# One group's softmax sums moved from ones-products to accumulating transfers, with a new hand-written order

## The chip, the cores and the metric

The kernel runs on one core of a Trainium2 chip. A core has five engines, each with its own queue of instructions, which it works through in order: PE (TensorE, matrix products), DVE (VectorE), ACT (ScalarE), POOL (GpSimd) and SP (SyncE, which here only issues transfers). Transfers run on 16 DMA engines. Instructions wait for each other by semaphores only. The metric is the device time of one execution in microseconds, the median of several runs.

## The reference

Two layers. The first is attention in which a query sees only the keys that fall to the same of 16 centroids; the second is a long convolution over the sequence by FFT, between two gates.

```python
# attention: batch 4, heads 8, seq 768, head_dim 64, 16 centroids per head
q_assign = argmax(einsum(q_n, c_n)); k_assign = argmax(einsum(k_n, c_n))
mask = q_assign[:, :, :, None] == k_assign[:, :, None, :]
scores = where(mask, scale * q @ k.T, -1e9)
attn = exp(scores - max); attn = attn / (sum(attn) + 1e-9)
x = (attn @ v) as (batch, seq, 512)
# gated convolution: d_model 512
x1, x2, x3 = split(x @ w_proj)
y = x1 * irfft(rfft(x2) * rfft(filter)) * x3
out = y @ w_out
```

## The kernel before

**Groups, pairs, key blocks.** The 32 heads of the four batches are worked through in 8 *groups* `n` of 4 heads (half a batch each); a group has two *pairs* `pr` of 2 heads. For a pair the 768 keys come in 6 *blocks* `sk` of 128. For each block PE makes the scores, keys on the partitions and the queries of both heads along the row, in three parts of 512 columns (`sc`); ACT turns each into exponentials (`p`, `exp`); PE multiplies the block with V into an accumulating pair of PSUM banks (`pv`, eight products, line 661). The mask is part of the score product: the one-hot rows of the assignments are extra rows of its operands (`aug`), copied there by small transfers `aug<-ohT` on SP (line 482). The assignments themselves come from `routing`: a similarity product (`sim`), then a run of DVE instructions up to `ohT`.

**The sums of the exponentials.** They have to be summed over all keys, over the six blocks and over the 128 partitions. Over the blocks: the first two are added in three thirds (`part`, line 678, on DVE or POOL), the other four one after another by DVE (`acc`, line 682, 128 x 1536 values). The accumulator `T.acc[os]` has one buffer for each pair of a group, so the same pair of the next group overwrites it. Over the partitions there are two ways:

- *late* groups (0, 1 and 7 before): a product with a matrix of ones on PE (`den`, line 695, four products, each in two instructions), a copy with the epsilon (`total`, lines 701 to 704), and for all but the very last pair two small transfers through DRAM, `dd<-den` and `dn<-dd` (lines 707, 709).
- other groups (2 to 6 before): a tree of three accumulating transfers issued by POOL (line 715): rows 64 to 127 are added onto rows 0 to 63, then 32 onto 32, then 16 onto 16, each waiting for the one before. The 16 rows left go to DRAM (`dd<-acc`, SP, line 719), come back spread over 128 partitions in pieces of 48 bytes (`dp<-dd`, SP, line 721), and DVE adds the 16 and the epsilon (`gather`, lines 725 and 726).

After either way DVE takes the reciprocal (line 728), SP writes it to DRAM (`dr<-dn`, line 729) and reads it back broadcast over 64 partitions twice (`rb<-dr`, line 732), and DVE scales the output by it into `xT` (line 761). The very last pair does this on PE instead (lines 743 to 761).

**The second layer.** When both groups of a batch have their `xT`, `hyena(b)` starts: projections (`U`, line 798; `G`), spectrum, inverse transform (`I`), output product (`W`). Its parts lie between the products of the following groups; those of the last batch lie behind all attention.

**The order.** `build` makes some 1,940 operations with their dependencies. The order of all of them is written out in `ORDER`, a word each: the letter is the engine (P, A, V, G, S for PE, ACT, DVE, POOL, SP), the number is the operation's number in `build`, and behind the colon stand the PSUM banks. An operation that may run on two engines gets its engine from there. The instructions are issued in this order, engine by engine, and the semaphores follow from the data that instructions share. The due times and costs in `build` do not act on the program once `ORDER` is given. The tables of the filter (`tables`) are loaded into the buffers of `y` and `y2`; `hot` warms up PE at the start with 16 products that read `y`.

Of the kernel before, what the change touches and what calls it, by code (L numbers as in the profile page):

```python
# [34 lines left out]
FIRST = 2  # L35
# [89 lines left out]
A35 V0 G18 S45 A46 P14:0 G29 S47 V22 P6:1 G20 S48 P5:2 G28 P11:3 S52 P1:4 G23 P2:5 V36 V53 S51 P16:6 G34 V37 P13:7 V59  # L125
G17 S49 V38 P4:0 V54 A39 A40 P7:1 V60 G19 V55 S50 P10:2 P3:3 G24 V61 P15:4 P9:5 P12:6 G137 V21 V56 P68:7 A66 A63 P70:0
V62 A57 P8:1 G33 S121 V41 A69 P74:2 G27 A58 P76:3 A64 G30 S124 A71 V26 P42:4 A77 V75 G65 S123 G72 P140:5 A67 P142:6
V43 P146:1 V143 S122 P82:7 G25 V141 G32 V44 S120 A73 P80:0 V83 G31 S135 A79 P102:3 V81 G78 P144:2 S134 P138:6 A103 V84
P96:5 A145 G136 S130 P100:4 V85 A97 P94:7 A101 V86 S131 P108:0 A95 G133 V87 A105 S127 P106:3 V88 A139 S126 V89 G104
P149:2 A99 P249:5 S128 G132 P251:4 A151 V93 V91 A250 V90 P243:7 A252 V92 S125 P183:6 V109 P245:5 A244 G98 V107 A184  # L130
S129 P185:0 P187:7 V150 G253 A186 P190:3 S288 V110 P192:6 P194:2 A188 V147 P200:0 V111 S287 A195 P202:7 V112 A246
P204:2 V199 A191 P189:45 V113 A193 V197 A201 A203 V198 P208:3 P210:6 A205 P212:0 V114 P216:7 P196 A211 V207 A209 A213
P218:2 P220:6 A254 P224:3 V148 P226:0 G154 V115 P206 A217 A219 V119 A118 P228:1 V153 P263:7 A116 V155 P214 V117 A221
V215 A248 P293:2 P222 A227 A294 V157 A229 P255:6 V223 A225 P257:0 P295:2 A264 P297:1 P300:3 A258 P261:7 A256 P302:0
V158 P230 A298 V160 A301 A262 V231 A296 P304:6 P310:1 S352 P312:3 A305 P267:72 S291 A303 V156 A232 S292 V159 A311
P233:6 S285 V269 A259 G162 P314:0 V268 S290 P318:1 A313 P299:45 V270 A315 G161 S289 A266 V234 P320:2 S286 P322:7 A319
V271 G152 P163:3 A323 S242 P171:0 A260 P164:6 S235 V272 P326:1 V273 G307 P328:7 A165 P306 A327 V166 A167 G358 P330:1
V274 A169 P316 G353 A331 V275 G309 A329 P334:3 P172:1 A321 V168 S278 P336:7 A175 G356 P177:2 V276 S280 V170 P324 A335
G308 S277 A173 V176 S279 V174 P419:361 S236 G247 A337 A181 V317 G357 A265 P338:0 P178:7 S453 A339 P332 S454 A421 V420
A422 V325 P359:0 A179 P361:1 P363:3 P340 A362 A360 V182 G426 A364 P366:6 V237 P368:1 A342 V180 P370:0 S238 G355 P376:3  # L140
P378:7 A371 V333 P365:45 S282 G354 A369 S455 A367 P380:2 A379 S283 P384:0 V374 P386:1 A381 P388:6 S281 P392:7 V341
A377 P372 S284 A387 S239 A385 P394:2 A389 S240 V375 P396:3 P343:1 A397 V373 A395 P427:063 V383 A393 A344 S345 P400:2
P402:7 A429 P404:1 V391 P382 A430 A428 A401 P461:0 A405 V399 P463:3 P465:6 A403 P390 A466 S346 A425 V407 P468:2
P435:17 S456 A464 V241 P470:6 P472:3 P398 A471 V437 A462 G476 V436 A473 P478:6 V438 P480:0 P482:1 P486:7 A481 P488:3
V347 P406 V439 A469 S348 A433 S458 V440 A483 P409:0 S418 V441 G475 A408 S459 P490:2 A489 P494:1 P467:45 V442 S460 A495
A487 S349 V443 G477 A410 P474 A479 A491 S446 V444 P496:3 S411 V485 P498:1 P502:7 A497 P701:062 S448 A434 S445 A424
V431 S447 P484 A499 V493 S350 S452 P504:3 P506:1 S457 P492 A505 V423 A704 S412 V501 A503 S520 P500 A507 S449 A703 S451
P639:3 V509 P508 A640 S738 A702 P641:7 V413 P643:1 A510 G708 P511:3 S414 A642 G432 P646:0 A644 V512 P648:2 P650:6 A647
G706 P656:7 S513 P658:1 A649 P660:3 P645:45 S450 V351 A657 A661 V653 A651 S416 P664:0 P666:2 A659 P668:7 V655 S415
P672:3 P674:6 A669 P676:1 V707 P652 A673 S514 V654 A677 A665 V663 P709:731 A675 A667 P680:0 V671 P682:6 S741 P684:2  # L150
A681 P662 A685 A711 V515 A683 V679 P743:0 S516 P670 A710 S740 A744 A712 S735 P745:2 V417 P747:6 P750:0 P752:1 P717:37
V687 A753 A746 S518 A748 S517 P754:1 A714 V718 P760:2 G689 P678 S736 V719 A755 G758 V720 S700 A751 P686 V721 P762:6
P764:3 A688 V722 P768:7 P770:1 P772:0 A761 V723 G757 P749:45 A765 A769 V724 P776:2 A771 P778:3 P780:7 P756 A779 V759
A763 V519 A705 G690 P766 V725 A781 V726 P521:1 S728 V767 S804 P523:3 A522 S729 A777 P531:6 S727 V525 A773 S732 V524
P526:7 A532 S730 V775 G691 P784:1 S739 P786:2 P528:0 A787 S742 A527 P533:3 A713 S734 V529 P788:6 P564:2 S733 V534 A789
S737 P774 V535 A785 G537 A715 V530 S692 A565 P805:7 V536 P807:6 P809:1 P812:3 A808 V539 P814:0 P816:2 A810 P782 V783
A806 A815 P822:6 A817 P824:1 P826:7 V538 A823 P830:0 P790 A813 V791 A831 A827 P540:2 S866 A792 P543:6 G819 V542 S693
P867:307 A825 V541 S731 V544 G821 P811:45 A869 V545 A870 V546 G793 A868 P548:1 V547 A873 P832:2 P834:6 V549 G716
P551:0 A833 P838:3 V550 P818 A835 G820 V552 A839 V553 P840:7 P842:2 V829 P875:163 A843 P556:0 V554 A877 S906 P828 A841
V837 A876 G794 A878 P846:2 P566:7 A847 V557 G555 P848:1 P850:3 V694 P909:6 P559:2 A910 P836 V695 V560 A851 S696 A871  # L160
V558 S903 G562 P911:6 V567 P568:3 S907 A912 V561 P913:0 P883:76 A569 G795 V845 S908 A879 S904 A849 P570:2 A914 S698
V884 G563 V885 P916:3 P918:1 P579:0 V886 A919 P920:6 P926:7 A580 P928:1 V887 A917 P844 A921 V853 A929 S796 P572:03
A927 P852 A573 V888 G855 V574 P930:6 G872 V575 P934:1 P581:7 A931 V889 A854 G576 S797 P936:0 P583:3 V582 A882 S901
P938:6 V890 P915:45 A584 A937 V891 G923 A939 P942:7 P922 A880 V571 S896 V577 A943 S894 V925 A874 P587:30 S697 V892
P585:6 V578 G856 S895 A588 A935 P932 S893 V586 G924 A881 S902 V589 V590 P944:2 S899 P946:7 V798 P950:1 P952:6 A947
S905 P594:0 V933 P596:3 A595 A951 P940 A953 V799 V941 S800 G857 A945 P954:7 S970 P1089:0 P598:1 A955 S898 A1090 V699
P1091:6 P1093:2 P1096:7 P1098:0 P948 V949 A1099 A1092 S801 A1097 P1100:0 S802 P1106:6 A1094 P956 V957 S858 A1107 A1101
P1108:7 P600:2 A958 V592 G959 P1110:6 V591 A1109 P1114:0 P1095:45 A599 G593 A1111 V601 V597 S859 P1116:7 P1118:1
P1151:623 A1117 G1105 A1115 A1119 P609:7 A1152 V1154 S1186 P602:01 A1153 V1103 S1187 P1159:236 V1104 A603 S897 A1158
V605 G1155 S900 V604 P1102 A1161 V1113 G960 S1191 A1162 S1190 A1160 P1122:0 P1124:1 A1123 P1167:23 S1192 V803 A610  # L170
G607 P1126:6 V1168 P1112 A1127 G606 V860 A1125 V1169 A1156 P1130:0 G961 P1132:7 V861 V1170 P1134:6 S862 A1131 P1193:1
P1195:2 P1197:3 P1120 A1196 V1121 A1135 A1198 P1200:0 A1133 P1202:2 V1171 P1204:6 P1210:3 A1194 P1212:7 P1128 A1203
S864 V1172 A1201 S1188 V1129 A1211 P611:1 S962 A1163 P1214:2 S863 P1218:0 A1166 P1220:3 V612 P1136 S1185 V1173 A1213
A1205 V1137 P1222:1 A1215 P613:7 A1138 P617:62 S963 A1221 P1199:45 V608 A618 S1189 A614 V1174 P1226:3 P1228:7 P1206
A1227 V620 G1208 A1223 V1175 A1219 P1230:3 V619 A1229 P1216 G1139 S1178 V1176 A1231 G622 S1177 A1157 V964 P1234:1
S1183 P615:0 A1164 V965 G621 P1224 S966 V616 S1180 V1207 S1179 P1236:2 V1209 P1232 A1237 V865 A1235 A1165 P1238:6 V623
P1325:730 S967 A1239 V1217 S968 G1140 P1317:216 S1150 A1328 S1182 A1326 V1225 A1327 S1254 P1240 A1320 S1184 A1319
S1181 A1318 P1255:0 V1233 P1257:3 P1259:7 A1256 P626:1 A1260 A1258 P624:2 P1262:6 V969 G1141 P631:0 A625 A627 V1241
P1264:7 P629:3 A1265 A1263 P981:2 V630 G1243 P971:1 V1321 P973:7 G1324 A972 S1142 A982 P983:6 G1323 V975 A1242 S628
V974 P976:3 A632 V984 P978:1 A977 V985 P1266:2 P1272:7 V979 P1014:0 A1267 S1143 V980 P1274:3 P1276:6 S1352 V987  # L180
P1280:2 A1275 P1261:45 G1244 A1273 V986 S1358 A1281 V988 A1015 S1356 P1282:1 P1284:3 V989 P990:7 A1283 S1351 P1288:2
G1269 P993:0 V991 A1289 P1016:1 S1355 V992 A1285 P1018:2 V994 A1277 G1270 S1316 P1020:7 V1017 A1019 V995 P998:3 G996
P1290:6 V1144 P634:1 V1145 V997 P1001:2 S1146 A635 P1006:0 V999 G1271 A1291 P1268 V1002 V1000 G1004 P636:1 V1003
P1292:6 V1021 P1296:3 G1005 P1009:2 V1007 P1298:7 P1278 V1010 A1299 G1245 A637 V1279 A1293 P1300:7 S638 P1029:1 A1301
# [1009 lines left out]
```

## Time and profile before

| | |
|---|---|
| median of 3 runs | 366.29 us (366.25 to 366.62) |
| the profiled execution's own time | 366.52 us |
| its span, first to last instruction | 364.7 us |
| granted TensorE clock, mean | 0.996 |
| busy: PE, DVE, ACT, POOL | 353.9, 339.3, 271.1, 137.1 us |

Busy time is the time in which an engine has an instruction under way. The products of PE are pipelined and their ends are modelled, so a busy PE may hide short waits; the chain of waits, followed back from the last instruction, tells what each step was released by. In the views by stretch each line gives start and end in us, the length, and then for PE, PEld (weight loads), DVE, ACT and POOL the busy time with the number of instructions, then the granted clock, the DMA engines' busy share and GB/s. In the groups by line, the figures after the bar are busy us, the mean ns of one instruction, and the idle time before them with what ended it.

### The profile page before, as it was taken

To read this page: it belongs to the slowest core of one execution; us is meant where nothing else is said; L and a number is where in the kernel's file an instruction comes from. 1 tells how busy PE (TensorE), PEld (TensorE's weight loads), DVE (VectorE), ACT (ScalarE), POOL (GpSimd) and SP (SyncE) were. 2 spreads that over 40 slices of the span, in tenths; PEclk is the share of its full clock that TensorE was granted. 3 is DMA by queue.
4 is the path that set the end of the run, shared out by engine and by line. 5 is a ranking of instruction groups with operands and counts; after the bars stand their busy time and mean duration, and the time that the engine had idled before them with its cause. 6 is when DMAs were issued, how large, how long until landed. Compare 5 with 4: busy or idle time off the path is not lost.

```text
span 364.7 us, 8483 instructions
## 1 busy us (share of the span) xinstructions
PE 353.9 (97%) x3254; PEld 198.8 (55%) x3254; DVE 339.3 (93%) x470; ACT 271.1 (74%) x502; POOL 137.1 (38%) x167
## 2 busy tenths in 40 slices
PE   8799999999999999999999999999999999999994
PEld 4445445454555555665565555555655556475771
DVE  8899889998999999989987999999999999999992
ACT  5999989789878777898987667789969826532232
POOL 8930841122131644344143463432340363045500
PEclk9999999999999999999999999999999999999998
DMA  9990999165576568678667948375755640410214
GB/s 171 226 248 14 218 180 179 26 166 132 120 134 147 102 108 129 130 148 151 131 125 193 174 111 155 43 156 56 178 80 155 89 61 17 162 43 2 117 59 173
DMA packets 88004, 45.69 MB, mean 125 GB/s; under 512 B 76488, under 2 KB 82012, under 8 KB 87964
## 3 DMA queue, kind: packets, MB, share of 16 engines
q1 hardware_dynamic: 84076, 35.16, 40.9%
q0 software_dynamic: 2960, 9.77, 18.6%
q8 instruction: 25, 0.41, 0.5%
q10 hardware_dynamic: 928, 0.23, 0.3%
q14 instruction: 15, 0.12, 0.1%
HBM read 31.59 MB, written 7.40 MB: 107 GB/s over the span
## 4 chain that ended last, share of the span: by engine, by line
PE 77%; DVE 9%; ACT 8%; DMA 3%; issue 2%; SPq 0%; DVEq 0%
PE bank L69 33%; PE pair L661 26%; PE bank L798 6%; PE bank L551 4%; ACT p L650 3%; DVE acc L682 3%; PE bank L583 2%; DMA dn<-dd 2%; PE bank L1015 2%; ACT aug L246 2%; ACT p L647 2%; PE bank L67 2%; DMA aug<-ohT 1%; PE bank L695 1%; PE bank L470 1%
## 5 line engine op out<-in xcount | busy, mean ns | idle before, releaser
L661 PE MATMUL pair<-p,vraw 128*64 128x385 f32 x768 | 140.4, 488 | 0.0
L650 ACT ACTIVATE p<-bank 128x512 f32<-128x512 f32 x192 | 108.5, 614 | 18.0 <-PE bank L69 15.6
L682 DVE TENSOR_TENSOR acc<-p,acc 128x1536 f32<-128x1536 f32 x64 | 112.1, 1751 | 2.1
L661 PEld LDWEIGHTS pair<-p,vraw 128*64 128x64 f32 x768 | 54.5, 136 | 47.6 <-issue 38.8
L69 PE MATMUL bank<-aug,aug 80*64 80x256 bf16 (+3 forms) x708 | 78.9, 327 | 1.3 <-DMA aug<-ohT 0.7
L647 ACT ACTIVATE p<-bank 128x512 f32<-128x512 f32 x96 | 57.8, 613 | 16.8 <-PE bank L69 11.3
L69 PEld LDWEIGHTS <-aug 80*64 80x64 bf16 (+1 forms) x708 | 40.9, 109 | 42.4 <-issue 29.7
L715 POOL DMA_DIRECT2D acc<-acc x30 | 24.1, 805 | 75.1 <-DMA acc<-acc 30.6
L678 POOL TENSOR_TENSOR acc<-p,p 128x512 f32<-128x512 f32 x23 | 29.8, 1298 | 48.6 <-ACT p L650 13.6
L69 PE MATMUL bank<-xT,wpj 128*64 128x384 bf16 x480 | 46.3, 326 | 0.0
L69 PEld LDWEIGHTS <-wpj 128*64 128x64 bf16 x480 | 27.6, 110 | 15.8 <-issue 5.3
L246 ACT CAST aug<-qkP 64x768 bf16<-64x768 f32 x43 | 35.4, 829 | 0.7
L246 ACT COPY qkP<-bank 128x512 f32<-128x512 f32 (+1 forms) x56 | 28.4, 562 | 7.9 <-PE bank L69 5.8
L69 PEld LDWEIGHTS <-y 128*64 128x64 bf16 x480 | 23.8, 110 | 11.5 <-issue 2.4
L822 DVE TENSOR_TENSOR tm<-bank,hm 128x512 f32<-128x512 f32 x44 | 27.9, 682 | 0.9 <-POOL y L826 0.2
L826 POOL TENSOR_TENSOR y<-tm 128x512 bf16<-128x512 f32 x17 | 21.5, 1275 | 13.9 <-DVE tm L822 8.7
L69 PE MATMUL bank<-wout,y 128*64 128x512 bf16 x192 | 23.1, 379 | 0.0
L798 PE MATMUL bank<-wpj,xT 128*64 128x512 bf16 x192 | 21.9, 379 | 0.0
L248 POOL CAST aug<-qkP 64x768 bf16<-64x768 f32 x17 | 13.9, 827 | 20.5 <-DVE dn L728 8.3
L246 ACT COPY ob<-bank 128x512 f32<-128x512 f32 x21 | 12.2, 594 | 11.0 <-PE bank L69 9.3
L900 POOL TENSOR_TENSOR y<-yy,x 128x768 bf16<-128x768 f32 x7 | 13.1, 1868 | 18.7 <-DVE yy L897 13.8
L551 PE MATMUL bank<-ident,qkraw 128*128 128x128 f32 x144 | 18.1, 276 | 0.0
(161 smaller groups left out, 447.2 us busy)
## 6 DMA issues: line engine op xcount, KB each, us to landing
qkraw<-in_k_dram SPq DMA_DIRECT2D x32, 192.0 KB
vraw<-in_v_dram SPq DMA_DIRECT2D x16, 384.0 KB
qkraw<-in_q_dram SPq DMA_DIRECT2D x31, 192.0 KB
rb<-dr SPq DMA_DIRECT2D x30, 192.0 KB
out_dram<-ob SPq DMA_DIRECT2D x11, 512.0 KB
acc<-acc POOLq DMA_DIRECT2D x10, 384.0 KB, 5.0
acc<-acc POOLq DMA_DIRECT2D x10, 192.0 KB, 3.9
wpj<-in_moe_w_proj_dram POOLq DMA_DIRECT2D x4, 384.0 KB, 6.3
```

The lines of the kernel that those rows point to most:

```text
L69: T.nc.tensor.matmul(out[64 * i:64 * i + 64], lhsT[:, 64 * i:64 * i + 64], rhs, start=start, stop=stop)
L246: T.nc.scalar.copy(out, in_)
L551: T.nc.tensor.transpose(bank(h.ids[i // 4])[:, block(i % 4, 2 < i < NT)], raw(ss[i // NT], i % NT), T.ident)
L647: T.nc.scalar.activation(o, ap(h).rearrange("p (a b) -> p a b", a=2), Act.Exp, scale=0.125)
L650: T.nc.scalar.activation(flat(s)[:, lo:lo + 512], ap(h), Act.Exp, scale=0.125)
L661: T.nc.tensor.matmul(o[64 * hp:64 * hp + 64, ch, :385], T.vraw[vs][:, hp, sk * D:(sk + 1) * D], T.p[slots[sk]][:, hp, 384 * ch:384 * ch + ...
L678: alu(e).tensor_tensor(o, x, y, op=Alu.add)
L682: T.nc.vector.tensor_tensor(T.acc[os], T.p[slots[sk]][:, :, :S], T.acc[os], op=Alu.add)
L715: op(("POOL", .8), lambda e, rows=rows: T.nc.gpsimd.dma_start(flat_()[:rows], flat_()[rows:2 * rows], accum_op=Alu.add), te, r=[], w=AK, b ...
L798: T.nc.tensor.matmul(ap(h)[64 * i:64 * i + 64], T.xT[xs][:, kt, tokens(m, i, w_)], T.wpj[:, kt, DM:2 * DM], start=kt == 0, stop=kt == ND - 1)
L822: op(("DVE", .68), lambda e, i=i, cs=cs, r=r, h=h: T.nc.vector.tensor_tensor(T.tm[r][:, cs], ap(h), hmrow(i, (0, 2, 2, 3)[2 * r + cs]), op ...
L826: op({"POOL": 1.3, "DVE": .68}, lambda e, i=i, r=r: alu(e).tensor_tensor(T.y[:, i, r], T.tm[r][:, 0], T.tm[r][:, 1], op=Alu.add if r else ...
```

## The change

Group 1 goes from the ones-product to the accumulating transfers: `FIRST`, below which a group is late, becomes 1. `LATE` writes the other end of that rule in pairs: pair 14 is the first of group 7, as before. `spread` takes the place of `last` where the very last pair is meant. The loads of the filter tables get a dependency on the 16 warm-up products. `ORDER` is new from the first word to the last: the order comes from a search whose picture of SP holds it back behind each load that spreads its rows.

```diff
-FIRST = 2
+FIRST, LATE = 1, 14
...
 ORDER = """
-A35 V0 G18 S45 A46 P14:0 G29 S47 V22 P6:1 G20 S48 P5:2 G28 P11:3 S52 P1:4 G23 P2:5 V36 V53 S51 P16:6 G34 V37 P13:7 V59
...
+A35 V0 G18 S45 A46 P16:0 G20 S48 V22 A47 G27 P11:1 S51 P14:2 G31 P4:3 S52 P1:4 G23 P15:5 V36 V59 S49 P13:6 G19 V37
...
 def tables(got):
...
-                   w=[("f", w_, e_)], byts=131e3 * (2 - e_), kind="load", after=got)
+                   r=[("hot", i) for i in range(HOT)], w=[("f", w_, e_)], byts=131e3 * (2 - e_), kind="load", after=got)
...
-                   r=["back"], w=[("f", w_, 1 + m)], byts=262e3 / m, kind="load", after=got)
+                   r=["back"] + [("hot", i) for i in range(HOT)], w=[("f", w_, 1 + m)], byts=262e3 / m, kind="load", after=got)
...
 def attention(n, pr, sins):
...
-        late = n == NG - 1 or n < FIRST
+        late = n < FIRST or 2 * n + pr >= LATE
+        spread = last and late
         if late:
             h, den_, dk = Bank(), lambda: T.den, ["den"]
...
-        if not last:
+        if not spread:
             if late:
                 op(("SP", .6), lambda e: T.nc.sync.dma_start(T.dd[os][:4, :384], den_()[0:128:32]), te + 2, r=dk,
...
 def hot():
...
-               r=["hot"], w=[h], alloc=h, free=[h])
+               r=["hot"], w=[h, ("hot", i)], alloc=h, free=[h])
```

Engine by engine the new order differs from the old one in where operations run, too. Of the 48 `part` sums DVE gets 33 instead of 25 and POOL 15 instead of 23. The two copies of mask rows of the first group that ACT made go to DVE, and one sum of the filter tables goes from POOL to DVE. A few copies of the second layer go from DVE to ACT, and single sums and products of it change between DVE and POOL. The `den` copy of group 0's first pair goes from DVE to ACT. Batch 0's first projection stands behind the third value product of group 3's first pair; before, it stood behind the third of group 2's second pair. The load of one quarter of `w_proj` (`wpj` 1) stands on POOL behind the tree of group 2's first pair; before, it stood just ahead of group 1's first value product.

210 lines of the change are left out of this document (105 added, 105 removed).

## The prediction

> **What bounds the kernel now.** I read the page first, then the engines' busy time by stretch, then the chain of waits.
>
> ```profile
> span 364.7 us, 8483 instructions
> PE 353.9 (97%) x3254; PEld 198.8 (55%) x3254; DVE 339.3 (93%) x470; ACT 271.1 (74%) x502; POOL 137.1 (38%) x167
> PE 77%; DVE 9%; ACT 8%; DMA 3%; issue 2%; SPq 0%; DVEq 0%
> ```
>
> PE is busy 97% of the span and carries 77% of the chain. DVE, at 93%, is close behind. Where each is short of full shows by stretch (busy us behind each length: PE, PEld, DVE, ACT, POOL):
>
> ```profile
> 0.00:16.00 16.00, 13.27 (x85) 6.49 (x85) 13.16 (x39) 12.03 (x23) 14.13 (x45) 1.00 1.01 196
> 16.00:56.00 40.00, 38.15 (x289) 19.61 (x287) 37.14 (x54) 38.15 (x71) 18.83 (x27) 1.00 0.80 165
> 56.00:316.00 260.00, 259.15 (x2353) 143.95 (x2351) 248.84 (x311) 205.78 (x380) 90.10 (x87) 1.00 0.62 122
> 316.00:365.00 49.00, 43.29 (x537) 28.76 (x533) 40.16 (x69) 15.13 (x30) 14.09 (x10) 0.97 0.23 85
> ```
>
> From 56 to 316 us PE idles under 1 us in 260 and DVE 11. So DVE is a second bound with little room, and both can be full together, as here (the same columns):
>
> ```profile
> 280.00:288.00 8.00, 8.00 (x80) 4.40 (x78) 7.90 (x10) 6.51 (x13) 2.31 (x3) 1.00 0.79 139
> 288.00:296.00 8.00, 8.00 (x68) 4.11 (x66) 7.97 (x14) 4.23 (x9) 3.28 (x4) 1.00 0.33 39
> ```
>
> Now the chain of waits (start, length, what), around the parts that change:
>
> ```profile
> 1.58 6.11 PE bank L1015 x15
> ...
> 48.61 6.45 DMA dn<-dd
> ...
> 55.91 1.67 DVE acc L682
> ...
> 69.42 0.97 DVE sim L588 x2
> 70.43 0.84 PE bank L69 x8
> ...
> 72.57 0.78 PE bank L695 x8
> ...
> 83.31 1.30 PE pair L661 x8
> 85.05 0.78 PE bank L695 x8
> ...
> 159.15 1.30 PE pair L661 x8
> ...
> 235.28 4.17 DMA aug<-ohT
> ```
>
> Three things are to be seen. From 56 to 70 us the chain runs through DVE's sums of exponentials: DVE is the bound there. From 70 us on it is PE nearly without a break, and the two ones-products of group 1 (L695, at 72.57 and 85.05) lie on it in full. At 235 us PE once waits for a mask transfer.
>
> For the working I laid the two orders side by side, gave every instruction the mean duration of its group in the trace, and took 0.05 us off each of DVE's: the durations of its 470 instructions add up to 365 us against 339.3 busy, since they overlap. The orders are then cut at the first value product of a pair. In before's trace these cuts are here (group 1; the last one of group 7), and at 159 us (group 4, in the chain above):
>
> ```profile
> 55.77 1.51 PE L661 MATMUL pair<-p,vraw 128*64 128x385 f32 x8
> ...
> 315.31 1.46 PE L661 MATMUL pair<-p,vraw 128*64 128x385 f32 x8
> ```
>
> From 55.77 to 159 (103.2 us) the order before holds 100.6 us of PE work and 98.7 of DVE work; DVE thus idles 4.5 us. From 159 to 315.3 (156.3 us) it holds 152.8 of PE and 150.2 of DVE.
>
> **The change part by part.** Removed and added, by their groups:
>
> ```profile
> L695 PE MATMUL bank<-acc,ones 128*32 128x384 f32 x48 | 5.1, 496 | 0.0
> L703 DVE TENSOR_SCALAR den<-bank 128x384 f32<-128x384 f32 x2 | 1.1, 552 | 1.1 <-ACT p L647 1.1
> L725 DVE TENSOR_REDUCE dn<-dp 128x12 f32<-128x192 f32 x10 | 4.8, 482 | 0.0
> L726 DVE TENSOR_SCALAR dn<-dn 128x12 f32<-128x12 f32 x10 | 3.4, 339 | 0.3
> L678 DVE TENSOR_TENSOR acc<-p,p 128x512 f32<-128x512 f32 x25 | 17.3, 717 | 0.2 <-ACT p L650 0.2
> L678 POOL TENSOR_TENSOR acc<-p,p 128x512 f32<-128x512 f32 x23 | 29.8, 1298 | 48.6 <-ACT p L650 13.6
> L715 POOL DMA_DIRECT2D acc<-acc x30 | 24.1, 805 | 75.1 <-DMA acc<-acc 30.6
> ```
>
> *PE* loses two ones-products, 2 x 0.78 = 1.56 us, nothing else: 344.6 us of work become 343.0.
>
> *DVE*: both of its den copies go, 2 x 0.55 = 1.1 us (group 1's with the product, group 0's to ACT, which loses group 1's other one). Two gathers come, 2 x (0.48 + 0.34) = 1.6 us. The new order gives DVE 33 of the 48 first sums (L678) instead of 25, 8 x 0.72 = 5.7 us; POOL loses 8 x 1.3. All other exchanges (mask rows and one table sum to DVE; copies, one fold and two products away from it) come to -3.3. In all +3.0 us: less work for the bound, more for the engine beside it.
>
> *Where DVE's load lands* decides. Between the cuts at groups 1 and 4 the new order holds the same PE work, 100.5 us (its dens gone, other work drawn forward), but 102.6 us of DVE work, 3.9 more. From group 4 to the last value product: PE 150.6 (2.2 less), DVE 150.5 (0.3 more). Behind it PE has 44.0 against 43.4, and DVE less. Up to group 1's cut the two orders have the same PE work, and DVE 52.3 against 52.1: no change, at a bound of 0.7 us either way, about what PE waits between 41 and 54 us now.
>
> *The sum* then has one unknown, i, DVE's idle time from group 1 to group 4. That stretch takes 102.6 + i in place of 103.2 if DVE sets it, and not less than PE's 100.5 with waits. Behind it I keep PE's 3.5 us of waits, so 2.2 us are saved, and the end costs 0.65. The change is i - 0.6 - 2.2 + 0.65 = i - 2.15 us. Its bounds: 0.5 (DVE 7.97 of 8 in the row at 288) and 4.5, what it idles now. I take 1.5, nearest the full rows, since 1.1 of the 4.5 is the den copy's own wait for ACT (L703) and goes with it. That gives -0.65 us: 366.52 of the profiled execution (span 364.7 and 1.8 around it) becomes 365.9; it stands 0.23 above the median of 366.29, so the time forecast is 365.6.
>
> *POOL and the DMA queues* get six accumulating transfers, with their landing times (KB, median us), and SP's waits behind them:
>
> ```profile
> acc<-acc POOLq DMA_DIRECT2D x10, 384.0 KB, 5.0
> acc<-acc POOLq DMA_DIRECT2D x10, 192.0 KB, 3.9
> acc<-acc POOLq DMA_DIRECT2D x10, 96.0 KB, 3.7
> ...
> wpj<-in_moe_w_proj_dram POOLq DMA_DIRECT2D x4, 384.0 KB, 6.3
> ```
> ```profile
> SPq L719 <- DMA acc<-acc: 18.6, 5, 8.8
> ...
> SPq L721 <- DMA dd<-acc: 9.1, 6, 2.6
> ```
>
> Six issues cost POOL 6 x 0.8 = 4.8 us, which its eight lost sums (10.4) pay for; POOL is 38% busy. The tree takes 5.0 + 3.9 + 3.7 = 12.6 us from issue to last landing, and the sum leaves the accumulator with dd, at most 2.6 us later. The accumulator alternates between pairs, so the same pair of the next group may write it only then. In the new order 18.8, 18.5 and 18.6 us of PE work lie between a tree's first issue and that next write, for group 1's two pairs and group 2's first: 3.3 us above 15.2. Hence cost nothing; without that cover DVE, which then holds most of these first sums, stands still. The two new dp loads hold SP as now; behind that of group 1's second pair stand the masks of group 3, with 3.2 us in between. One projection weight's load moves from just before group 1's first value product to behind the tree of group 2's first pair on POOL; 10.6 us of PE work lie between it and the first projection, against 6.3 to land. The first projection of batch 0 itself moves 12.3 us of PE work later, behind the longer way of group 1's sums. The `hot` edges tell only the order what the stored data demand anyway: the warm-up products end at 7.7 us (chain), the tables are wanted later, nothing. `LATE` and `spread` give for 8 groups exactly what stood there.
>
> [...]
>
> **Rivals.** *DVE becomes the bound in groups 1 to 3.* Slower. Place: its queue between 56 and 159 us. It decides from i = 2.15 on; where its idle stays at 4.5, the change is +2.35: 368.6 us. For it: the chain already runs through DVE from 56 to 70 us, and 3.9 us are added to 4.5 of room. Against: the full rows at 280 to 296.
>
> *A tree is late.* First to third issue on POOL, an ordinary tree and the slowest:
>
> ```profile
> 243.15 0.81 POOL L715 DMA_DIRECT2D acc<-acc  x1 [6.67 <-DVE acc L682]
> ...
> 252.79 0.77 POOL L715 DMA_DIRECT2D acc<-acc  x1 [3.52 <-DMA acc<-acc]
> ```
> ```profile
> 196.97 1.00 POOL L715 DMA_DIRECT2D acc<-acc  x1 [5.21 <-PE bank L69]
> ...
> 203.63 0.76 POOL L715 DMA_DIRECT2D acc<-acc  x1 [3.88 <-DMA acc<-acc]
> 205.94 2.50 POOL L678 TENSOR_TENSOR acc<-p,p 128x512 f32<-128x512 f32 x2 [1.54 <-ACT p L647]
> ...
> 214.35 0.75 POOL L715 DMA_DIRECT2D acc<-acc  x1
> ```
>
> 9.6 and 17.4 us; the new order leaves 10.8 to 11.9. A tree as slow as the second, 6.4 us late against the 11.0 of group 1's second pair, outruns the cover of 3.3 by 3.1 and holds DVE's first sums, and on SP group 3's masks: 365.6 + 3.1 = 368.7. It decides from 4.0 us of lateness on (3.3 + 0.65). Against: it was held by POOL's own sums, and the new order keeps these out of the three early trees save one.
>
> *It is hidden anyway*: DVE takes back what PE is spared (i = 2.15), 366.3.
>
> *All of it is had*: i at 0.5 and group 6's wait of about a microsecond at 235 us gone too (its masks now have 3.9 us of PE work ahead of the score instead of 2.8): 365.6 - 1.0 - 0.5 = 364.1.
>
> **How the numbers follow.** Forecast (365.6, own range 365.0 to 366.2) 0.46; all of it 0.13; hidden 0.09; DVE the bound 0.21; a tree late 0.11. A measurement of this kernel tells 0.2%, 0.73 us, from no change. The forecast's centre lies at that edge: 0.28 of its 0.46 falls below 365.56, 0.18 within. So faster 0.28 + 0.13 = 0.41; same 0.18 + 0.09 = 0.27; slower 0.32. The range goes from 364.2, just above the case that has it all, to 368.2, which takes in most of DVE's case and a tree late by less than the slowest, and leaves out the far end of both.
>
> **What would show it.** Right: the L695 group shrinks from 48 to 32 products, 36 accumulating issues, L678 at 33 on DVE and 15 on POOL; DVE busy near 342 us, between 248 and 252 of 256 to 260 in the long middle stretch; PE's waits of group 1 gone from the chain. Wrong: PE idle that grows by over 2 us between 56 and 160 us, with the chain on DVE (the first rival) or on acc<-acc, dd or aug<-ohT transfers (the second); or group 6's masks waiting as before. A head that reaches group 1's first value product more than 0.7 us off 55.8 would undo the first term.

## The result, and the profile after

| | before | after |
|---|---|---|
| median, us | 366.42 (366.18 to 367.33, 9 runs) | 369.60 (367.33 to 373.37, 9 runs) |
| the profiled execution's own time, us | 366.52 | 373.12 |
| its span, us | 364.7 | 371.3 |
| busy PE, DVE, ACT, POOL, us | 353.9, 339.3, 271.1, 137.1 | 357.6, 340.5, 272.4, 132.0 |

The ratio of after to before is 1.0065 [1.0039, 1.0091], which is 2.4 us: slower, by 3.2 us in the medians of the table. The ratio leaves out the two longest executions of after (373.12 us, the one profiled, and 373.37), which lie over 1.5% above its fastest; the other seven have a median of 368.41 us. The forecast was 365.6 us, the range ended at 368.2. Another profiled execution of the same kernel, at 370.8 us (run 1 below), has its losses at the same places.

The page of after, its first lines, shares of the chain, and groups:

```profile
span 371.3 us, 8500 instructions
...
PE 357.6 (96%) x3249; PEld 207.6 (56%) x3249; DVE 340.5 (92%) x475; ACT 272.4 (73%) x508; POOL 132.0 (36%) x164
...
PE 83%; ACT 9%; DMA 3%; DVE 2%; issue 1%; SPq 1%; POOL 0%; DVEq 0%; ACTq 0%
...
L716 POOL DMA_DIRECT2D acc<-acc x36 | 28.7, 798 | 110.0 <-DMA acc<-acc 50.5
...
L678 POOL TENSOR_TENSOR acc<-p,p 128x512 f32<-128x512 f32 x15 | 19.1, 1275 | 25.8 <-ACT p L647 6.8
L678 DVE TENSOR_TENSOR acc<-p,p 128x512 f32<-128x512 f32 x33 | 21.4, 684 | 6.7 <-ACT p L650 5.5
```

(After's lines stand one higher than before's from the ones-product on: L716 is the old L715.) The change does what it says: 36 accumulating issues, first sums 33 on DVE to 15 on POOL, 32 ones-products left (L696). DVE's share of the chain fell from 9 to 2%. But PE is busy 3.7 us longer with 1.56 us less to do. By stretch, after and then before (length, then busy PE, PEld, DVE, ACT, POOL, the granted clock, DMA share, GB/s):

```profile
16.00:56.00 40.00, 36.95 (x260) 17.59 (x261) 35.62 (x52) 36.73 (x69) 14.44 (x22) 0.96 0.84 172
56.00:104.00 48.00, 45.94 (x368) 23.48 (x364) 43.34 (x44) 42.46 (x79) 12.83 (x14) 0.96 0.69 133
104.00:122.00 18.00, 16.03 (x111) 8.14 (x109) 16.89 (x20) 10.17 (x20) 3.41 (x5) 0.91 0.80 139
122.00:320.00 198.00, 197.96 (x1860) 119.23 (x1858) 189.16 (x253) 152.41 (x282) 74.90 (x71) 1.00 0.63 123
```
```profile
56.00:104.00 48.00, 47.90 (x392) 23.80 (x390) 45.49 (x46) 41.74 (x80) 9.48 (x10) 1.00 0.57 127
104.00:122.00 18.00, 18.00 (x160) 10.04 (x156) 17.70 (x21) 14.92 (x29) 4.62 (x6) 1.00 0.54 123
122.00:316.00 194.00, 193.26 (x1808) 110.11 (x1807) 185.65 (x246) 149.12 (x274) 76.00 (x73) 1.00 0.64 121
```

All is lost ahead of 122 us. Behind it PE does not wait in 198 us; group 6's mask wait is gone as well. Ahead of it PE idles 7.1 us in 106 (3.05, 2.06 and 1.97), and the granted clock is 0.91 to 0.96 where it was 1.00.

To add up both I use one measure below, **lost time**: from the start of a value product (L661) in the trace I take the time that all PE instructions ahead of it need at their undisturbed length (in all 344.6 us before, 343.0 after). What grows from one value product to the next was lost there, in waits or to a slower clock. Lost in each stretch, us, for the executions profiled:

| up to the first value product of | before | after | after, another execution |
|---|---|---|---|
| group 0 | 4.4 | 4.4 | 4.9 |
| group 1 | 3.5 | 5.8 | 5.8 |
| group 2 | 1.4 | 2.3 | 2.3 |
| group 3 | 0.7 | 6.9 | 4.1 |
| group 4 | 0.6 | 1.0 | 1.0 |
| last value product | 3.5 | 2.4 | 2.4 |

Two stretches stand out, the ones that end with the first scores of group 1 and of group 3. Here is after's chain of waits through both (start, length, what):

```profile
45.15 0.59 ACT tm L442
...
45.85 0.76 DVE hm L446
...
50.48 4.97 DMA aug<-ohT
...
58.32 2.56 PE pair L661 x8
...
63.77 1.30 PE pair L661 x8
```
```profile
108.52 1.91 DVE acc L678 x3
...
110.45 0.37 DVE ohT L608
...
113.00 5.33 DMA aug<-ohT
...
119.86 2.55 PE pair L661 x8
...
123.71 1.30 PE pair L661 x8
```

Both times the chain goes through the last steps of a one-hot on DVE, which stand behind something else (a table sum that waits for ACT; three first sums), then through a mask transfer of 24 KB that takes about 5 us in the chain. And both times eight value products behind the wait take 2.56 us in place of 1.30 (in the other execution only at group 1). PE's waits add up to this (total, times, longest, us):

```profile
PE bank L69 <- DMA aug<-ohT: 3.3, 4, 1.4
...
PE bank L69 <- DVE sim L588: 1.6, 1, 1.6
```

What landed so late stands on POOL's queue and on SP's, after:

```profile
111.54 0.83 POOL L1006 DMA_DIRECT2D wpj<-in_moe_w_proj_dram  x1
```
```profile
108.46 0.59 SPq L722 DMA_DIRECT2D dp<-dd  x1
110.83 2.76 SPq L482 DMA_DIRECT2D aug<-ohT  x4
```

The weight quarter that the change moved is issued among group 3's masks, and the new read-back `dp` of group 1's second pair stands ahead of them, 2.4 us from issue to issue.

### The profile page after: what moved, and what is told of

The parts are those of the page before. It is cut to its first block, busy times and chain, and to the rows that moved or that the text cites. A ratio compares the mean times of both kernels' runs of the same rounds, so it can differ in the third digit from the quotient of the medians.

```text
span 371.3 us, 8500 instructions
## 1 busy us (share of the span) xinstructions
PE 357.6 (96%) x3249; PEld 207.6 (56%) x3249; DVE 340.5 (92%) x475; ACT 272.4 (73%) x508; POOL 132.0 (36%) x164
## 4 chain that ended last, share of the span: by engine, by line
PE 83%; ACT 9%; DMA 3%; DVE 2%; issue 1%; SPq 1%; POOL 0%; DVEq 0%; ACTq 0%
PE bank L69 36%; PE pair L661 29%; PE bank L799 6%; PE bank L551 4%; ACT p L650 3%; DMA aug<-ohT 3%; PE bank L583 2%; PE bank L67 2%; ACT qkP L246 2%; PE bank L1016 2%; ACT p L647 1%; ACT aug L246 1%; PE bank L470 1%; ACT tm L442 1%; PE bank L696 1%
## 5 line engine op out<-in xcount | busy, mean ns | idle before, releaser
L661 PE MATMUL pair<-p,vraw 128*64 128x385 f32 x768 | 143.9, 498 | 0.0
L650 ACT ACTIVATE p<-bank 128x512 f32<-128x512 f32 x192 | 110.2, 621 | 23.7 <-PE bank L69 16.1
L661 PEld LDWEIGHTS pair<-p,vraw 128*64 128x64 f32 x768 | 56.1, 139 | 49.3 <-issue 42.3
L716 POOL DMA_DIRECT2D acc<-acc x36 | 28.7, 798 | 110.0 <-DMA acc<-acc 50.5
L647 ACT ACTIVATE p<-bank 128x512 f32<-128x512 f32 x96 | 58.5, 619 | 12.0 <-PE bank L69 7.5
L69 PEld LDWEIGHTS <-wpj 128*64 128x64 bf16 x488 | 30.8, 110 | 13.5 <-issue 4.7
L246 ACT CAST aug<-qkP 64x768 bf16<-64x768 f32 x44 | 36.2, 828 | 0.7
L246 ACT COPY qkP<-bank 128x512 f32<-128x512 f32 (+1 forms) x57 | 28.6, 557 | 8.7 <-PE bank L69 5.3
L69 PEld LDWEIGHTS <-y 128*64 128x64 bf16 x512 | 26.1, 110 | 11.1 <-issue 2.6
L678 POOL TENSOR_TENSOR acc<-p,p 128x512 f32<-128x512 f32 x15 | 19.1, 1275 | 25.8 <-ACT p L647 6.8
L678 DVE TENSOR_TENSOR acc<-p,p 128x512 f32<-128x512 f32 x33 | 21.4, 684 | 6.7 <-ACT p L650 5.5
L685 ACT COPY osb<-pair 128x770 f32<-128x770 f32 x16 | 13.2, 827 | 10.7 <-PE pair L661 10.5
L246 ACT COPY x<-bank 128x384 f32<-128x384 f32 x23 | 10.9, 483 | 10.6 <-PE bank L69 9.9
```

Source lines behind the costliest of these rows:

```text
L69: T.nc.tensor.matmul(out[64 * i:64 * i + 64], lhsT[:, 64 * i:64 * i + 64], rhs, start=start, stop=stop)
L246: T.nc.scalar.copy(out, in_)
L647: T.nc.scalar.activation(o, ap(h).rearrange("p (a b) -> p a b", a=2), Act.Exp, scale=0.125)
L650: T.nc.scalar.activation(flat(s)[:, lo:lo + 512], ap(h), Act.Exp, scale=0.125)
L661: T.nc.tensor.matmul(o[64 * hp:64 * hp + 64, ch, :385], T.vraw[vs][:, hp, sk * D:(sk + 1) * D], T.p[slots[sk]][:, hp, 384 * ch:384 * ch + ...
L678: alu(e).tensor_tensor(o, x, y, op=Alu.add)
```

## The experiments

Three theories stand at the start. **W**: the moved weight quarter holds the masks back. **D**: DVE is the bound in groups 1 to 3. **T**: a tree is late. All ratios are against the kernel before on the same chip.

| run | median, us | lowest to highest | ratio [95%] |
|---|---|---|---|
| 1 after, again | 369.88 | 367.92 to 372.32 | 1.0092 [1.0058, 1.0126] |
| 2 first weight quarter early | 367.59 | 366.49 to 369.31 | 1.0035 [1.0021, 1.0049] |
| 3 two quarters moved | 367.42 | 366.26 to 373.11 | 1.0037 [1.0016, 1.0057] |
| 4 before, with a load beside masks | 366.41 | 366.17 to 367.42 | 1.0005 [0.9995, 1.0015] |
| 5 = 2, one-hot of group 1 first | 369.03 | 368.35 to 369.72 | 1.0066 [1.0050, 1.0081] |
| 6 = 5, gather behind | 369.42 | 367.92 to 370.18 | 1.0071 [1.0050, 1.0091] |
| 7 before, tree for one pair | 374.05 | 373.95 to 374.39 | 1.0207 [1.0193, 1.0220] |
| 8 = 2, one-hot of group 1 first, mended | 367.28 | 365.46 to 368.72 | 1.0018 [1.0001, 1.0036] |
| 9 = 8, gather behind | 366.92 | 366.09 to 368.67 | 1.0021 [1.0008, 1.0035] |
| 10 = 8, one-hot of group 3 first | 366.55 | 365.69 to 368.97 | 1.0013 [0.9998, 1.0027] |
| 11 = 10, masks ahead of read-back | 367.44 | 367.19 to 368.72 | 1.0029 [1.0018, 1.0041] |
| 12 = 10, similarity first | 367.32 | 366.35 to 372.17 | 1.0027 [1.0010, 1.0044] |
| 13 = 12, read-back behind masks | 366.67 | 365.95 to 368.96 | 1.0021 [1.0003, 1.0038] |
| 14 = 13, ones-product later | 367.24 | 366.43 to 371.32 | 1.0034 [1.0012, 1.0055] |
| 15 = 14, second quarter moved too | 367.65 | 366.90 to 370.80 | 1.0042 [1.0023, 1.0062] |

**1 to 4: the weight load.** Run 1 is the changed kernel once more.

> The changed kernel once more, for a second profile and its spread. Theory W (weight loads on POOL's queue hold the mask transfers of groups 1 and 3 back, PE waits at those groups' first scores, and its granted clock is lower for a while behind each wait): 367 to 373 us again, with the waits of the chain on aug<-ohT before the first scores of groups 1 and 3, and a clock below 1.00 only behind these. Theory D (DVE, with 3 to 4 us more work between groups 1 and 4, is the bound): DVE full there, PE's waits on DVE's copies and sums, no tie to transfers.

Run 1 waits for masks at groups 1 and 3 again (0.58 and 0.78 us, 1.30 and 0.90 us). The lower clock behind these waits, which W expected, stands only at group 1 (0.91 from 45 to 64 us; from 84 to 122 us it is 1.00), and there is a lower clock before 24 us, too (0.93), behind a wait of 1.0 us for DVE's `aug`.

Run 2 moves one word of the order, run 3 a second one:

```diff
 POOL's queue
 acc  (first sum, group 1, pair 0)
+wpj  (quarter 1)
...
 tree (16 rows, group 2, pair 0)
-wpj  (quarter 1)
```

> Changed kernel; the load of one quarter of w_proj that stands behind the tree of group 2's first pair is issued some 50 us earlier, behind POOL's first sum of group 1. All else as it was. W: group 3's masks land in about 2 to 3 us instead of 5.3, the 4 us of PE waits between 114 and 124 us go: 2 to 4 us faster than the changed kernel, 365 to 367, ratio to before 0.998 to 1.003. D: no difference from the changed kernel, 1.006. Theory T (a late tree of group 1 holds DVE's first sums and SP): no difference either.

> As the one before, and the load of another quarter, which is issued at 48.8 us among the masks of group 1, stands behind POOL's first sum of group 1 too. W: the wait of 2.8 us before group 1's first value product shrinks as well, 364.5 to 366 us, ratio 0.995 to 0.999. D and T: 1.006 as the changed kernel.

Run 2 gains 2.3 us on run 1, and its interval lies wholly below run 1's. Against the first measurement of after (1.0065 [1.0039, 1.0091]) it gains 1.1 us by the ratios, and the intervals overlap. The loss up to group 3's first value product falls from 4.1 to 1.7 us in the profiles. Of the waits for masks one is left in its profile, and that is group 1's; group 3's first scores, which waited 1.40 us in after, start without a wait (after, then two lines of run 2):

```profile
118.47 1.39 PE L69 MATMUL bank<-aug,aug 128*64 128x256 bf16 x10 [1.40 <-DMA aug<-ohT]
```
```profile
54.34 2.98 PE L69 MATMUL bank<-aug,aug 80*64 80x512 bf16 x22 [1.54 <-DMA aug<-ohT]
...
112.34 1.26 PE L69 MATMUL bank<-aug,aug 80*64 80x512 bf16 x14
```

So W holds for group 3: DVE's order and the trees were left as they were, and the masks were not issued earlier against PE's need (5.2 us before PE was done with the work ahead of these scores in after and in run 1, 4.9 us in run 2). Run 3 takes the other quarter from beside group 1's masks. The mask wait of 1.54 us goes there too, but the time doesn't change: PE now waits at the same two products for ACT's exponentials (0.53 us) and DVE's last sum (0.97 us). The masks were not the only thing late. Still, group 1's first value product now starts at 55.91 us; it was at 55.77 in the kernel before and at 58.06 in after.

Run 4 makes the same collision in the order before, with the load of `w_out` issued beside group 2's masks:

```diff
 POOL's queue
-wout
...
 acc  (last first sum, group 1, pair 1)
+wout
```

> The kernel before with one load moved: w_out (as much data as a quarter of w_proj and a third more) is issued on POOL at about 76.6 us, beside the masks of group 2, instead of 43. Nothing else changes, and its first reader comes much later. W: the masks of group 2 land late and PE waits before that group's first scores, 1 to 4 us slower than before, ratio 1.003 to 1.011, with more spread. D and T: no difference, 0.999 to 1.001.

Nothing: 1.0005. Group 2's masks are issued there from 75.6 us on and wanted at about 83 us, so that even held up by some us they come in time; when they landed is not in the trace. A missed number, and it narrows W: here, where the masks had 7 us to land, the load cost nothing.

**5 to 9: DVE's queue.** Runs 5 and 8 let group 1's one-hot pass the table sum that waits for ACT. In run 5 that sum stands behind the next scaled table as well, and reads that one's values from the shared buffer; so runs 5 and 6, which is built on it, do not compute what the reference asks for.

```diff
 5 and 8, DVE's queue
 m    L602
-hm   L446 (waits for ACT)
 oh   L603
 ohT  L606
+ohT  L608
+hm   L446
 hm   L446
-ohT  L608
```

> Group 1's masks. On top of the moved first weight quarter (367.59 us, ratio 1.0035): the two table sums of DVE that wait for ACT's scaled tables (L446) go behind the transposed one-hot (L606, L608) of group 1 instead of before it. Theory Q (DVE's queue makes group 1's masks late): the masks are issued about 1.5 to 2 us earlier than 47.65 us, TensorE's lost 2.8 us at group 1's first value product falls below 1.0 us, and the median falls to 364.5 to 366.0 us, below the kernel before. Rival L (the masks' landing is slow whenever they are issued there, because of what else is in flight): still over 2 us lost, 367.2 to 367.8 us. Rival D (DVE has too much to do there, the wait only goes elsewhere): the lost time up to group 1's second value product stays within 0.5 us, 367.0 to 367.8 us.

> The run before this one with one more edit: the sum over the 16 read-back rows and the reciprocal of group 1's first pair (L727, L728, L729) go behind group 3's two similarity transposes (L588) in DVE's queue. Theory: they held TensorE's wait of 0.4 us there (1.0 us lost with the lower clock behind it), so that goes, and the time falls by 0.4 to 1.0 us. Rival: the first sum ahead of both (L682) holds the transposes anyway, change under 0.2 us.

> Group 1's masks once more, on top of the moved first weight quarter (367.59 us, 1.0035): the one-hot's last three steps (L603, L606, L608) go ahead of the first table sum that waits for ACT (L446), and that sum stays ahead of the scaled table that takes its buffer, so only three instructions of DVE change their place. Theory Q (DVE's queue made the masks late): issued by about 46.0 us instead of 47.65 us, the 2.8 us lost at group 1's first value product fall below 1.0 us, 364.5 to 366.0 us, below the kernel before. Rival A (ACT's scaled tables are late there too, so the loss only moves to the table products and the first sums): 2 us or more are lost between 45 and 64 us, 367.0 to 368.5 us.

> The same, with the sum over the 16 read-back rows and the reciprocal of group 1's first pair (L727, L728, L729) behind group 3's two similarity transposes (L588). If those held TensorE's bank wait of 0.4 us at group 2's fifth value product, the 0.95 us lost there go: 0.5 to 1.0 us below the run without it. If DVE's last sum ahead of both holds it: within 0.2 us of it.

Run 5 is no fair test of Q: the sum waited 3.1 us for ACT, and the tables behind it came late. In run 6 the wait for the similarity is 0.44 us where run 5 has 1.1, and a wait of 1.4 us for group 3's masks is new. Run 8 is the fair one. First SP's line of group 1's masks in after, then the same line in run 8, then what run 8's PE waits for there:

```profile
48.50 3.16 SPq L482 DMA_DIRECT2D aug<-ohT  x5
```
```profile
45.60 3.15 SPq L482 DMA_DIRECT2D aug<-ohT  x5
```
```profile
53.74 1.88 PE L69 MATMUL bank<-aug,aug 80*64 80x256 bf16 x12 [0.53 <-ACT p L650]
...
59.07 0.85 PE L696 MATMUL bank<-acc,ones 128*32 128x384 f32 x8 [0.63 <-DVE acc L682]
```

The masks are issued 2.9 us earlier than in after and nobody waits for them. Yet 1.5 us are still lost at group 1's first value product and 0.9 at the next, 2.4 in place of run 2's 2.9. Theory Q has the masks right and the sum wrong; rival A, that ACT's work is late there too, has most of it. Against the kernel before, however, this is no longer a loss: group 1's first value product starts at 55.43 us, 0.3 ahead of before, which lost as much a little earlier. The median is 0.3 us below run 2's, less than the intervals can tell. Run 9 moves the sum over 16 rows, and PE's wait for the similarity stays (0.75 us): DVE's last sum ahead of both holds it, the rival; its 0.4 us below run 8 is within the spread. A wait of 1.4 us for group 3's masks is new here, too.

**7: the tree alone,** in the order before, for group 1's first pair:

```diff
-        late = n == NG - 1 or n < FIRST
+        late = n == NG - 1 or n < FIRST or (n, pr) == (1, 1)
```

(with `FIRST = 1`, and the six operations of the tree put into the old order.)

> The tree alone: the order of the kernel before, in which only group 1's first pair is summed by the three accumulating loads (its ones-product, copy and two small loads go; three issues on GpSimd, two loads, the sum over 16 rows come; no other work changes its place except this pair's reciprocal, spreading loads and table product, and the second pair's loads that share their tiles). Theory O (the order alone is what made the change slower; the tree itself gives TensorE its product back): 365.3 to 366.0 us, against 366.4 before, with no wait at 45 to 58 us. Theory N (a tree in group 1 gives nothing, as its cost on DVE and in loads eats the product): 366.2 to 366.8 us. Theory T (a tree here is late or disturbs the masks): above 366.8 us, with a new wait of TensorE between 85 and 115 us.

Theory T, in the hardest form, and for a reason that I had not seen. The tree's own sum is in time, but the next pair shares the small tiles `dn` and `rb` with it, so its loads follow late, and its table product comes after batch 0's first projection wants it. DVE, then PE's wait:

```profile
112.04 1.02 DVE L761 SCALAR_TENSOR_TENSOR xT<-osb,rb 128x768 bf16<-128x768 f32 x1 [4.50 <-DMA rb<-dr]
```
```profile
PE bank L798 <- DVE xT L761: 4.9, 1, 4.9
```

One wait of 4.9 us; the median is 7.7 above before. That would explain why the changed kernel's order has batch 0's projection so much later; no run tried it. It also gives the price of a wait, below.

**10 to 15: group 3 and the read-back.**

```diff
 10, DVE's queue
+ohT  L608 (group 3)
 acc  L678 x3
-ohT  L608 (group 3)
 12, DVE's queue
+sim  L588 x2 (group 3)
 acc  L682
 dn   L727, L728, L729
-sim  L588 x2 (group 3)
 11 and 13, SP's queue
-dp   L722 (group 1, pair 1)
 aug  L482 x4 (group 3)
+dp   L722 (group 1, pair 1)
 13, DVE's queue
-dn   L727, L728, L729
 qkP  L248
+dn   L727, L728, L729
```

> On top of both mended places (first weight quarter early, group 1's one-hot first: 367.28 us, but its executions spread from 365.5 to 368.7 us where those of the kernel before spread from 366.2 to 366.7 us): in DVE's queue the last step of group 3's one-hot (L608) goes ahead of the three first sums (L678) of group 2's second pair. Theory M (group 3's masks come out just about when TensorE wants them, so that some executions wait for them and some don't): issued about 1.9 us earlier, the spread shrinks to under 1 us and the median falls to 365.3 to 366.0 us, 0.4 to 1.1 us below the kernel before. Rival S (the spread is from somewhere else, such as group 1's or the first loads): 366.8 to 367.7 us, as wide as before.

> The same, and on SyncE four of group 3's masks (L482) go ahead of the load that reads back 16 rows of group 1's second pair (L722, 2048 pieces of 48 bytes). Theory M with the read-back's packets ahead of the masks on their way: another 0 to 0.5 us and the tightest spread of all. Rival: once the masks are issued early enough, the read-back costs nothing, within 0.2 us of the run without it; if the later read-back makes the pair's sum late on DVE (L727, first instruction at about 110 us), 0.5 to 2 us slower.

> The version with the three mended places (366.55 us), and group 3's two similarity transposes (L588) go ahead of the last sum (L682) and of the sum over the 16 read-back rows (L727, L728) of DVE's queue, which they had to wait behind for about 2.3 us after TensorE's product was done. Theory D3 (in groups 2 and 3 it is the place in DVE's queue that makes TensorE wait, 1.0 us and some 1.5 us with the lower clock): the loss at group 2's fifth value product falls below 0.4 us, and the median to 365.0 to 365.8 us, below the kernel before. Rival (DVE as a whole is what holds that stretch, so the same wait comes back at the next product): within 0.4 us of 366.55 us.

> On top of the run with the similarity transposes first (367.32 us; the wait they had to bear is gone there, but TensorE waits 1.3 us for group 3's masks again, whose four issues took 4.6 us behind the read-back of 2048 pieces of 48 bytes): that read-back (L722) goes behind the four masks (L482) in SyncE's queue, and the sum over its rows (L727, L728) with the reciprocal behind group 4's first copy (L248) in DVE's. Theory P (the tree's small pieces on SyncE's queue hold the masks): the four issues take under 2.8 us, no wait of TensorE over 0.5 us is left between 84 and 122 us, and the median falls to 365.0 to 366.0 us, below the kernel before. Rival (a stretch with two trees, their read-backs and the masks has no order without such a wait): another wait of 1 us or more there, 366.8 to 368 us.

Run 10 brought the median to 366.55 us, no longer to be told from before (1.0013 [0.9998, 1.0027]), but the spread stayed: theory M isn't shown by it. Run 11 put the read-back behind the masks and lost: DVE's queue has the sum over the rows ahead of group 4's copy, and PE then waits 1.2 us for that copy, the rival's last clause. Run 12 freed the similarity from its wait, and the masks' wait came back in its place. Its lines of SP, and the one of PE:

```profile
105.77 0.68 SPq L722 DMA_DIRECT2D dp<-dd  x1
106.55 4.61 SPq L482 DMA_DIRECT2D aug<-ohT  x4
```
```profile
113.26 1.28 PE L69 MATMUL bank<-aug,aug 80*64 80x512 bf16 x14 [1.25 <-DMA aug<-ohT]
```

Run 13's SP lines:

```profile
104.78 2.60 SPq L482 DMA_DIRECT2D aug<-ohT  x4
107.42 0.58 SPq L722 DMA_DIRECT2D dp<-dd  x1
```

Four masks right behind the read-back take 4.61 us to issue, the first of them 2.71; ahead of it they take 2.60, the first 0.55, and nothing waits for them. With runs 6 and 9 that makes three runs in which group 3's masks are late without the weight load beside them: the load is one cause of that wait and not the only one. The loss up to group 3's first value product is 1.1 us in run 13 (0.7 before). So theory P holds for the issue and for the wait; the time, 0.65 us below run 12, stays within overlapping intervals, and the expected 365 to 366 us were not reached: 3.1 us are lost from there to group 4's first value product (0.6 before), where among others the later table product makes PE wait 0.6 us. The rival of that run, that no order of this stretch is without a wait, is nearer the result.

> On top of the last version (366.67 us, two thirds of its executions at 366.0 to 366.9 us, one third at 368.4 to 369.0 us): the ones-product of group 0's second pair (L696) goes behind the next two score products of TensorE's queue, as it waited 0.6 us there for DVE's last sum (0.86 us lost). Theory: the loss at that place falls below 0.4 us and the faster executions come 0.3 to 0.8 us lower, 365.2 to 366.4 us. Rival: the next score or value product waits in its place, unchanged within 0.3 us.

> The same, and the second weight quarter that is issued beside group 1's masks (at 47.3 us, its packets at 48 to 51 us) goes behind the quarter that was moved before (57 us). Theory W for group 1 (now that its masks are issued early, that quarter is what makes some executions wait for them): the third of the executions at 368.4 to 369.0 us goes, and all lie within 1 us of the fastest. Rival: they stay, so they come from somewhere else, such as the lower clock that some executions show at the first value products.

```diff
 14, PE's queue
-ones-product L696 (group 0, pair 1)
 scores x2 (group 1)
+ones-product L696 (group 0, pair 1)
 15, POOL's queue
-wpj  (quarter 2, at 47 us)
...
 wpj  (quarter 1)
+wpj  (quarter 2)
```

Both missed. In run 14 the wait for DVE's sum is gone and ACT's exponentials hold the next scores in its stead (three waits, 1.2 us, after two of 0.8). In run 15 the longer executions stay.

## Why the prediction was wrong

**What was right.** The counts. PE's work of 343.0 us. DVE near its old busy time (340.5; I had said 342). The end: from group 4's first value product on, the changed kernel takes 153.1 us where before took 156.3, a gain of 3.3 where I had 2.2, with group 6's wait gone. These terms are there; they are lost earlier.

**The step that cost most: the moved weight quarter, put at nothing.** I set its 6.3 us of landing against its own reader, 10.6 us of PE work away, and its reader indeed never waited. I did not ask what else was in flight where it was put. Those were group 3's masks. Run 2 prices it: 2.3 us against run 1, 1.1 against the first measurement, either more than the whole gain forecast.

**"The two new dp loads hold SP as now", "with 3.2 us in between".** In after the masks come 2.4 us behind the read-back, where their four issues take 2.76 us; in run 2, also at 2.4 us, they take 3.05, and nothing waits for them. So at that distance the read-back alone made no wait. It holds only at that distance: where they come 0.1 us behind its end on the same queue, the first mask takes 1.94 us to issue (run 10, without a wait of PE) or 2.71 (run 12, with one of 1.25); with the read-back put behind them it takes 0.55 (run 13).

**"Up to group 1's cut", "no change, at a bound of 0.7 us either way".** Group 1's first value product starts at 58.06 us, 2.3 late. I compared sums of work (PE equal, DVE 52.3 against 52.1) and took the order within them for harmless. ACT, whose queue I did not lay out, copies three parts of `qkP` (L246) ahead of and between the scaled tables in the new order; DVE waits for ACT with the one-hot behind that wait in its queue. After's DVE lines, then the same step before:

```profile
45.85 0.75 DVE L446 SCALAR_TENSOR_TENSOR hm<-bank,hw,tm 128x512 bf16<-128x512 f32 x1 [2.59 <-ACT tm L442]
...
49.20 0.36 DVE L608 TENSOR_SCALAR ohT<-ohT 64x768 bf16<-64x768 bf16 x1
```
```profile
46.63 0.43 DVE L608 TENSOR_SCALAR ohT<-ohT 64x768 bf16<-64x768 bf16 x1
```

Run 3 and run 8 each take the mask wait away. Both leave ACT's and DVE's lateness under it, but their first value product of group 1 starts within 0.4 us of before's, inside the bound of 0.7. So the late masks are what that term left out. That ACT's copies are its root was only read from the trace, and not tried.

**i, DVE's idle time between groups 1 and 4.** I took 1.5 us, with 4.5 as the bound. In the mended runs 10 and 13 that stretch takes 106.0 and 106.4 us, so by the prediction's own 102.6 us of DVE work i is 3.4 and 3.8; in after's other execution it is 107.9, i = 5.3, past the bound. The bound was wrong in kind: it supposed that DVE is either working or free, while here both DVE and PE wait for a third party (ACT, a mask) at once. With 3.4 to 3.8 the formula i - 2.15 gives +1.3 to +1.7; the further 1.1 us of gain behind group 4 brings the mended kernel to about the time of before, where runs 10 and 13 are. So between half of the loss (1.1 of the 2.4 us of the first measurement, by the ratios) and two thirds of it (2.3 of the 3.5 us of run 1 over before) is the collision of the weight load with group 3's masks, shown by run 2; the rest, with the saving itself, is given back in groups 1 to 3, at one place or the next. Rival by rival: "DVE the bound" had the size (368.6) and not the mechanism, since run 2 gained time with DVE's work and order as they were; "a tree is late" did not occur in after (12.2, 10.4 and 9.8 us from first to third issue for the three early trees; a tree's first transfer lands in 5.5 us there, in 5.0 before), although its sign, a chain on `aug<-ohT`, did; "hidden anyway" (366.3) is what the mended versions come to.

**A wait was priced at its length.** It cost more here. Run 7's one wait of 4.9 us took 7.4 us of lost time. After, whose PE idles 5.1 us more than before from 16 to 122 us (7.1 against 1.85, 0.10 and 0.00), loses 9.4 us more up to group 3's first value product; run 1's profile, with 4.0 us more of idle time, loses 7.1 us more. The difference fits the half clock that these profiles show, below: PE was busy at half clock for 7.6 us in after up to that value product and for 4.7 us in run 7, and half of each is 3.8 and 2.4 us, beside differences of 4.3 and 2.5.

**What stays open.** No run was clearly faster than before, so that a tree in group 1 brings anything is not shown; the fastest single execution of run 8 (365.46 us) lies 0.7 us under the fastest of before on that chip (366.16). Some executions of runs 10 and 13 (five and four of twelve) are 1 to 3 us longer than the rest, and run 15 shows that the second weight quarter isn't why. The mean granted clock of an execution goes with this (those of before have 0.995 to 1.000, whatever their time). In run 13 the eight at 365.95 to 366.92 us have 0.997 to 1.000, the four at 368.38 to 368.96 us 0.992 or 0.993; in run 10 the seven up to 366.71 us have 0.997 to 1.000, the five from 367.17 us on 0.987 to 0.995. So in the longer ones PE ran longer at half clock, if 0.50 is the only lower rate in them, as it is in the traces of before and after; in run 13 longer than in any execution of before. Where in the program that was is not shown, as the profiled executions of both runs are short ones. The four shortest of run 8, at 0.998 to 1.000, took 365.5 to 365.7 us, the time forecast; as they are picked by their time, they show no gain.

## What to carry to other kernels

When a transfer is moved, its own reader is half of the question: list what else is on the way at the new place, the small transfers with little slack first, and what stands behind it in the issuing queue. Lay out every engine's queue around a moved stretch, not the two busiest: equal sums of work say nothing about a queue in which one late instruction stands ahead of what others need. In a kernel with one engine at 97% a saving on it only shows where nothing else is late; here taking one wait away uncovered the next four times (runs 3, 8, 12, 14). Where the executions of one order spread wider than usual, compare their granted clocks, too.

## What the hardware showed that was not expected

**A short wait of PE can be followed by half the clock.** The granted clock by stretch: after, around the waits of 0.57 and 1.40 us, the second of which ends at 118.47 us; run 7, around its wait of 4.9 us (length, PE busy, clock, DMA share, GB/s; the last line of each is cut where the clock changes):

```profile
114.00:118.00 4.00, 2.50 (x18) 1.00 0.75 130
118.00:120.00 2.00, 1.53 (x12) 0.71 0.07 12
120.00:122.00 2.00, 2.00 (x8) 0.50 0.71 218
122.00:124.00 2.00, 2.00 (x22) 0.94 0.72 119
...
118.84:122.25 3.41, 3.41 (x18) 0.50 0.44 135
```
```profile
108.00:113.00 5.00, 0.21 (x2) 0.80 0.67 120
113.00:116.00 3.00, 2.89 (x14) 0.50 0.08 18
116.00:118.00 2.00, 2.00 (x12) 0.54 0.68 223
118.00:122.00 4.00, 4.00 (x42) 1.00 0.54 126
...
111.00:117.83 6.83, 4.72 (x24) 0.50 0.38 87
```

The clock is at half for 3.41 us in after, for twice that in run 7, and then full again. That length is a step in the traces of after and before, whose clock records hold 1.00 and 0.50 and nothing else: every change of the granted clock lies a whole multiple of 3.41 us behind the start of full clock (by 4, 5, 15, 16, 33, 34 and 107 steps in after's trace, by 104 in before's). That start lies 6.20 us from the first instruction in after and 7.09 us in before. After's steps at half clock, the one behind 355 us left out, begin at 19.85, 57.40 and 118.84 us, and in the steps just ahead of them PE was busy 69, 61 and 42% of the time by the profile. From 98.36 to 101.77 us it was busy 65%, and full clock follows, so the busy share alone doesn't decide it. Nor is the fall certain at one place: behind the same wait of 0.95 us, which ends at 18 us, run 12 shows 0.56 from 21 to 24 us and run 10 1.00 (run 12, then run 10):

```profile
21.00:24.00 3.00, 3.00 (x11) 0.56 1.21 213
```
```profile
21.00:24.00 3.00, 3.00 (x27) 1.00 1.19 231
```

That costs run 12 1.1 us with nothing else changed there: its eight value products from 21.33 us on take 2.64 us, run 10's from 21.06 us on 1.52. In runs 10 and 13 the longer executions are those with the lower mean clock, as given above; why some orders leave more of it was not tested. Ahead of the half clock stood 2.0 us of waiting with work between in after and 0.95 us in run 12; in run 10 the same 0.95 us brought none.

**Masks landed later beside a load of another queue.** The third mask of group 3 (24 KB) landed in 4.3 us in after and in 4.6 in run 1, beside the weight quarter from POOL's queue; in run 2, without it, in 3.0 us. The fourth mask of group 1, issued at 49.6 us in runs 2 and 3 alike, landed in 4.8 us with the second quarter beside it (run 2) and in 1.9 us without it (run 3). The quarter isn't all there is: in run 15 that mask, issued at 48.1 us, took 4.7 us without it. By what way a load would hold a mask up was not shown.
